# Chunked attention and two MoE layers: C loaded as half the bytes, in two transfers per unit into four tiles cleared once

## Chip, cores and metric

One core of one Trainium2 chip. The metric is the device time of one execution in microseconds (us), the median of several runs. The engines are TensorE (PE), VectorE (DVE), ScalarE (ACT), GpSimd (POOL) and SyncE (SP), which here only issues transfers.

## What is computed

Three layers in a row. The first is a chunked linear attention over x (4 batches, 8 heads, 768 steps, head size 32), with decays a and the projections B and C (16 numbers per step and head):

```python
for c in range(nc):
    cum = np.cumsum(la, axis=-1)
    L = np.exp(cum[:, :, :, None] - cum[:, :, None, :]) * causal
    CB = np.einsum('bhin,bhjn->bhij', Cc, Bc)
    y_intra = np.einsum('bhij,bhjd->bhid', CB * L, xc)
    y_inter = np.einsum('bhin,bhnd->bhid', Cc, state) * decay_to_i[:, :, :, None]
    y[:, :, sl] = y_intra + y_inter
    state = decay_full[:, :, None, None] * state + np.sum(Bx, axis=2)
```

The second is a gated MLP on the 3072 tokens (256 to 1536 and back, silu), the third routes each token to one of 8 experts (256 to 1024 and back, relu) by a gate with a bias per modality. C enters the first layer alone, in CB and in y_inter.

## The kernel before

The attention runs in 24 units (NU) of 128 steps of one batch with all 8 heads. A block is four units, 512 tokens; there are six, and the MLP of a block follows its four units. The order of all instructions is written out by hand: `first_block` (L807) has the setup, the loads of the first four units and the first two blocks, `block` (L950) the others, where the pieces of the next units are set between the groups of MLP matmuls. Each engine runs its own part of this order, one instruction after the other.

`load(u)` (L160) issues on SP's queue, for one unit, first xbb (256 KB: x, B by step, B transposed) and then cbd (256 KB: C). Both have four buffers, so unit u+4 is loaded when the values of unit u are done. In the first block SP's order is: at (L174), load(0), load(1), the rest of at (L812), load(2), weights 0 of the MLP (L391, 768 KB each), load(3), weights 1, and then load(u + 4) after each unit; the constants c1 go out on ACT's queue meanwhile (L175).

C comes as a block diagonal matrix, made on the host: a partition is one (group of 4 heads, head in the group, n), its free index (half of the unit, 4 heads, 64 steps), and all but the partition's own head are zeros. 64 KB of the 256 KB are numbers of C. `scores_mm` (L281) multiplies it with B transposed at L297, 64 partitions by 256 columns, so that each head meets only itself; `values_mm` (L331) multiplies single heads' 64 columns of it with the state at L353. `scores_m` (L301) masks the scores, `weigh` (L273) makes xw = x times a decay on POOL or DVE, `emit_d` and `emit_u` (L249, L264) make the decays du and U for a block. On POOL the order in the start is weigh(1), emit_d(0), emit_d(1), weigh(2), weigh(3), weigh(4). `decode` (L396) turns the packed weights into numbers on ACT and DVE (ha at L403); on ACT ha of the first weights stands ahead of the states st of unit 1 (L326, L327), which PE reads at L353.

`setup_ones` (L213) writes r16 and r32, the operands that sum or spread over groups of heads; r16 goes into cum_ends (L238).

Of the kernel before, what the change touches and what calls it, by code (L numbers as in the profile page):

```python
# [9 lines left out]
F32 = mybir.dt.float32  # L10
# [10 lines left out]
NB, NH, S, D, N = 4, 8, 768, 32, 16  # L21
NC = S // 128
NU = NB * NC
# [16 lines left out]
C_P8 = C_MU + 8  # L40
# [13 lines left out]
def _consts():  # L54
    k = np.arange(128)[:, None]
    j = np.arange(128)[None, :]
    c = np.zeros((128, C_END), np.float32)

    same = k // 64 == j // 64
    m = np.zeros((128, 128), np.float32)  # L60
    m[same & (k % 64 < 32) & (k > j)] = 1.0
    m[same & (k % 64 >= 32) & (k <= j)] = -1.0
    c[:, C_S:C_S + 128] = m
    for q, (lo, hi) in enumerate(((32, 96), (96, 128), (0, 32))):
        c[lo:hi, C_S + 128 + q] = -1.0
    r = np.arange(128)
    c[:, C_ME] = (r // 32) % 2
    for q in range(8):
        c[:, C_MU + q] = 4 * (r // 64) + (r // 8) % 4 == q
    c[:, C_P8:C_P8 + 8] = (r % 8)[:, None] == np.arange(8)[None, :]  # L70
    c[:, C_MK:C_MK + 64] = j[:, :64] >= k % 64
    c[:, C_ID:C_ID + 128] = k == j
    c[:, C_TRI:C_TRI + 128] = k < j
    e = np.arange(E)
    c[:, C_IE:C_IE + 8] = 8 - e
    for g, (b0, n) in enumerate(GROUPS):
        c[:, C_EC + 8 * g:C_EC + 8 * g + 8] = E * b0 * BLK + e * (n * BLK)
    c[:, C_LE:C_LE + 64] = (e[None, :] <= e[:, None]).reshape(1, 64)
    c[:, C_TT:C_TT + 11] = np.arange(11)
    c[:, C_KK:C_KK + 4] = np.arange(4) * BLK  # L80
    c[:, C_IO:C_IO + 8] = e
    return c


def _layout(inp):
    o = {}
    at = inp["a"].reshape(NB * NH, NC, 128).reshape(NB, NH, NC, 128).transpose(3, 0, 2, 1)
    o["at"] = at.reshape(128, NBLK, 32)
    xk = inp["x"].reshape(NB, NH, NC, 128, D).transpose(3, 0, 2, 1, 4).reshape(128, NU, DM)
    bk = inp["B"].reshape(NB, NH, NC, 128, N).transpose(3, 0, 2, 1, 4).reshape(128, NU, 128)  # L90
    bt = inp["B"].reshape(NB, NH, NC, 128, N).transpose(1, 4, 0, 2, 3).reshape(128, NU, 128)
    o["xbb"] = np.concatenate([xk, bk, bt], axis=2)

    ct = inp["C"].reshape(NB, 2, 4, NC, 2, 64, N).transpose(1, 2, 6, 0, 3, 4, 5).reshape(2, 4, N, NU, 2, 64)
    cd = np.zeros((2, 4, N, NU, 2, 4, 64), np.float32)
    for h in range(4):
        cd[:, h, :, :, :, h] = ct[:, h]
    o["cbd"] = cd.reshape(128, NU, 512)
    o["cst"] = _consts()

    def bits(w):
        return np.ascontiguousarray(w).view(np.int64)

    wg = bits(inp["moe_w_gate"]).reshape(2, 128, NF, 128).transpose(2, 1, 0, 3)
    wv = bits(inp["moe_w_val"]).reshape(2, 128, NF, 128).transpose(2, 1, 0, 3)
    wo = bits(inp["moe_w_out"]).reshape(NF, 128, DM)
    o["mw"] = np.concatenate([wg.reshape(NF, 128, 256), wv.reshape(NF, 128, 256), wo], axis=2)
    o["mid"] = np.ascontiguousarray(inp["moe2_modality_id"]).reshape(NU, 128).T
    o["wl"] = inp["moe2_w_gate"].reshape(2, 128, E).transpose(1, 0, 2)
    o["mb"] = np.broadcast_to(inp["moe2_modality_bias"].reshape(1, 2, E), (128, 2, E))  # L110
    w1 = inp["moe2_w1"].reshape(E, 2, 128, F2).transpose(0, 2, 1, 3).reshape(E, 128, 2 * F2)
    w2 = inp["moe2_w2"].reshape(E, NF2, 128, DM).transpose(0, 2, 1, 3).reshape(E, 128, NF2 * DM)
    o["ew"] = np.concatenate([w1, w2], axis=2).reshape(E * 128, 4096)
    return {k: np.ascontiguousarray(v) for k, v in o.items()}
# [3 lines left out]
def kernel(  # L118
# [5 lines left out]
    nc = tc.nc  # L124
# [6 lines left out]
    ap_ = att_stack.enter_context(tc.tile_pool(name="ap", bufs=1, side="right"))  # L131

    def ps_a(shape, name):
        return ps.tile(shape, F32, tag="a", bufs=3, name=name)

    def ps_g(name, shape=(128, BLK)):
        return ps.tile(list(shape), F32, tag="g", bufs=3, name=name)
# [5 lines left out]
    c1 = ap_.tile([128, C1], F32, name="c1")  # L143
# [6 lines left out]
    r16 = ap_.tile([128, 128], F32R, name="r16")  # L150
    r32 = ap_.tile([128, 2, 128], F32R, name="r32")
    mk = c1[:, C_MK:C_MK + 64]
    raw = {}
    xt_t = {}
    y_t = {}
# [4 lines left out]
    def load(u):  # L160
        if u >= NU or u in raw:
            return
        r = {}
        xbb = ap_.tile([128, 512], F32, name="xbb", tag="xbb", bufs=4)
        nc.sync.dma_start(out=xbb, in_=I["xbb"][:, u])
        r["x"] = xbb[:, 0:DM].rearrange("k (h d) -> k h d", h=8)
        r["b"] = xbb[:, DM:DM + 128]
        r["bt"] = xbb[:, DM + 128:]
        r["c"] = ap_.tile([128, 2, 4, 64], F32, name="cbd", tag="cbd", bufs=4)
        nc.sync.dma_start(out=r["c"].rearrange("p r h i -> p (r h i)"), in_=I["cbd"][:, u])  # L170
        raw[u] = r

    def setup_loads():
        nc.sync.dma_start(out=at0[:, 0:2], in_=I["at"][:, 0:2])  # L174
        nc.scalar.dma_start(out=c1, in_=I["cst"][:, 0:C1])  # L175
        nc.scalar.preload_act_table_set("natural_log_exp_and_others")

    def setup_ln(b0, b1):
        a = at[:, b0:b1]
        nc.vector.tensor_scalar(out=a, in0=at0[:, b0:b1].unsqueeze(2).to_broadcast([128, b1 - b0, 2, 32]),  # L180
                                scalar1=1e-6, scalar2=1.0, op0=ALU.max, op1=ALU.min)
        nc.scalar.activation(out=a, in_=a, func=AF.Ln)
# [28 lines left out]
        nc.scalar.activation(out=t, in_=c1[:, C_ME:C_ME + 1], func=AF.Silu)  # L211

    def setup_ones():  # L213
        p8 = c1[:, C_P8:C_P8 + 8].unsqueeze(2)
        nc.vector.tensor_copy(out=r16.rearrange("p (h n) -> p h n", h=8), in_=p8.to_broadcast([128, 8, 16]))
        nc.vector.tensor_copy(out=r32.rearrange("p g (h i) -> p (g h) i", h=4), in_=p8.to_broadcast([128, 8, 32]))

    def cum_split(b0, n):
# [62 lines left out]
    def scores_mm(u):  # L281


        r = raw[u]
        r["pc"] = [ps_a([128, 512], "pc") for _ in range(2)]
        r["pS"] = [p[:, 256:320] for p in r["pc"]]
        for q in range(4):
            for i in range(2):
                if i == 0 or u % NC != NC - 1:
                    k = slice(64 * i, 64 * i + 64)  # L290
                    nc.tensor.matmul(out=r["pS"][i][32 * q:32 * q + 32], lhsT=r["b"][k, 32 * q:32 * q + 32],  # L291
                                     rhs=r["xw"][k, 2 * q:2 * q + 2], start=True, stop=True,
                                     tile_position=(64 * i, 32 * q))
        for q in range(4):
            for g in range(2):
                k = slice(64 * g, 64 * g + 64)
                nc.tensor.matmul(out=r["pc"][g][32 * q:32 * q + 32, 0:256], lhsT=r["bt"][k, 32 * q:32 * q + 32],  # L297
                                 rhs=r["c"][k, q // 2].rearrange("p h i -> p (h i)"), start=True, stop=True,
                                 tile_position=(64 * g, 32 * q))

    def scores_m(u):  # L301
# [29 lines left out]
    def values_mm(u):  # L331

        r = raw[u]
        st = s_t.pop(u)
        py = r["py"] = [ps_a([128, 192], "py"), ps_g("py", (128, 192))]
        for g in range(2):
            for q in range(4):
                for i in range(2):  # L340
                    k = slice(64 * i, 64 * i + 64)

                    nc.tensor.matmul(out=py[i][32 * q:32 * q + 32, 128 * g:128 * g + 64], lhsT=r["xw"][k, 4 * g + q],  # L343
                                     rhs=r["m"][k, g, q], start=g == 0, stop=True, tile_position=(64 * i, 32 * q),
                                     skip_group_check=True)
        for half in range(2):
            if half == 0 and u % NC == 0:
                continue
            for q in range(4):
                for g in range(2):  # L350
                    k = slice(64 * g, 64 * g + 64)
                    o = 64 * (half + g)
                    nc.tensor.matmul(out=py[g][32 * q:32 * q + 32, o:o + 64],  # L353
                                     lhsT=st[k, half, 32 * (q % 2):32 * (q % 2) + 32], rhs=r["c"][k, half, q],
                                     start=False, stop=True, tile_position=(64 * g, 32 * q), skip_group_check=True)

    def values_out(u):
# [743 lines left out]
    with tc.For_i(bounds[0], bounds[1], 1) as t:  # L1101
        r = Routed(2, t, hl_t[0], None)
# [34 lines left out]
```

## Time and profile before

| what | value |
|---|---|
| median of 3 runs | 530.3 us (530.1 to 530.32) |
| the profiled execution's own time | 530.17 us |
| its span in the profile | 528.4 us |
| PE matmul busy | 505.0 us, 96% of the span |
| DVE, ACT, POOL busy | 289.1, 219.5, 105.8 us |
| transfers | 45.55 MB, 86 GB/s over the span |
| xbb and cbd | 24 transfers each, 256 KB |

The profile is of one execution. Times in it are us from the start of the span, where not marked ns. A line L297 is line 297 of the kernel. A busy PE is not PE at its peak: matmuls overlap, and their ends are modelled. Who released a wait is inferred from semaphore events. "issue" is time in which an engine waited for nothing that the profile shows. SPq is SP's queue, PEld PE's weight loads, PEldq its queue.

### The profile page before, as it was taken

How to read it: one execution, taken by the hardware profiler on the slowest of the kernel's cores; microseconds unless marked ns; L12 is line 12 of the kernel's file. 1: busy time of each engine (PE TensorE's matmuls, PEld its weight loads, DVE VectorE, ACT ScalarE, POOL GpSimd, SP SyncE). 2: the span in 40 equal slices, each digit the busy share in tenths (PEclk: the TensorE clock that was granted, in tenths of full speed). 3: DMA queues.
4: the chain of work that ended last, by engine and by line, in shares of the span. 5: the costliest groups of instructions: out<-in, count | busy, mean ns of one | idle time of the engine just before them, and what ended most of it. 6: DMA issues, size and time to landing. Idle time of an engine off the chain costs nothing.

```text
span 528.4 us, 11243 instructions
## 1 busy us (share of the span) xinstructions
PE 505.0 (96%) x4580; PEld 416.7 (79%) x4580; DVE 289.1 (55%) x631; ACT 219.5 (42%) x403; POOL 105.8 (20%) x127
## 2 busy tenths in 40 slices
PE   6889999999999999999999999999999999999990
PEld 3677787778788778888788778888899989999880
DVE  4998786944554544445444554455466564646320
ACT  4785575434333334233333332434454353534220
POOL 3200000220220130005000224211055426240220
PEclk9999999999999999999999999999999999999995
DMA  8954422011230312012100104234188544521100
GB/s 299 338 183 137 155 80 82 25 49 41 82 32 30 103 15 66 3 47 74 21 2 2 43 1 158 84 121 41 41 105 176 162 130 137 153 104 42 40 22 22
DMA packets 20694, 45.55 MB, mean 86 GB/s; under 512 B 4768, under 2 KB 8352, under 8 KB 20640
## 3 DMA queue, kind: packets, MB, share of 16 engines
q1 hardware_dynamic: 17424, 38.29, 26.2%
q0 software_dynamic: 3072, 6.41, 4.1%
q8 instruction: 37, 0.61, 0.6%
q14 instruction: 17, 0.14, 0.1%
q10 hardware_dynamic: 144, 0.11, 0.1%
HBM read 38.30 MB, written 6.50 MB: 85 GB/s over the span
## 4 chain that ended last, share of the span: by engine, by line
PE 76%; issue 11%; DVE 4%; POOL 3%; ACT 2%; DMA 1%; SPq 0%; POOLq 0%; DVEq 0%; ACTq 0%
PE py L469 19%; PE pg L441 18%; PE pv L441 18%; PE ph L758 7%; PE po L779 6%; PE pt L553 2%; POOL out L793 2%; PE pc L297 2%; PE py L353 1%; PE py L343 1%; PE pc L291 1%; DMA xbb<-in_xbb 1%; PE pu L270 1%; DVE wv L412 1%; PE px L747 1%
## 5 line engine op out<-in xcount | busy, mean ns | idle before, releaser
L441 PE MATMUL pg<-xt,wh 128*128 128x512 f32 x288 | 93.2, 404 | 0.3 <-ACT xt L374 0.2
L441 PE MATMUL pv<-xt,wh 128*128 128x512 f32 x288 | 90.4, 395 | 0.0
L449 DVE TENSOR_TENSOR h<-h,pv 128x512 f32<-128x512 f32 x72 | 49.4, 686 | 66.7 <-PE pv L441 55.6
L456 DVE TENSOR_TENSOR hl<-h,hh 128x512 fp32r<-128x512 f32 x72 | 50.2, 697 | 61.7 <-ACT hh L455 61.5
L758 PE MATMUL ph<-xt,hl 128*128 128x512 f32 x288 | 72.7, 394 | 0.0
L779 PE MATMUL po<-hl,hh 128*128 128x256 f32 x384 | 70.1, 283 | 0.0
L441 PEld LDWEIGHTS pv<-xt,wh 128*128 128x128 f32 x288 | 54.2, 188 | 12.8
L779 PEld LDWEIGHTS po<-hl,hh 128*128 128x128 f32 x384 | 60.3, 188 | 2.1
L455 ACT CAST hh<-h 128x512 fp32r<-128x512 f32 x72 | 44.6, 620 | 40.4 <-DVE h L449 40.4
L441 PEld LDWEIGHTS pg<-xt,wh 128*128 128x128 f32 x288 | 52.1, 188 | 11.6 <-ACT xt L374 0.6
L448 ACT ACTIVATE h<-pg 128x512 f32<-128x512 f32 x72 | 42.7, 593 | 41.7 <-PE pg L441 41.7
L614 POOL DMA_INDIRECT slots<-ids,si x24 | 26.0, 1081 | 168.4 <-DVE si L606 163.6
L758 PEld LDWEIGHTS ph<-xt,hl 128*128 128x128 f32 x288 | 51.7, 188 | 9.2
L469 PE MATMUL py<-hh,wh 128*128 128x512 f32 x144 | 58.7, 407 | 0.0
L441 PE MATMUL pg<-xt,wl 128*128 128x512 f32 x144 | 57.0, 396 | 0.3 <-DVE wl L421 0.3
L469 PE MATMUL py<-hl,wh 128*128 128x512 f32 x144 | 56.9, 395 | 0.0
L469 PE MATMUL py<-hh,wl 128*128 128x512 f32 x144 | 56.8, 394 | 0.0
L441 PE MATMUL pv<-xt,wl 128*128 128x512 f32 x144 | 56.8, 394 | 0.0
L779 PE MATMUL po<-hl,hl 128*128 128x256 f32 x192 | 53.9, 281 | 0.2 <-DVE hl L767 0.2
L767 DVE SCALAR_TENSOR_TENSOR hl<-ph,hh 128x512 fp32r<-128x512 f32 x48 | 33.0, 688 | 31.8 <-ACT hh L766 30.8
L766 ACT ACTIVATE hh<-ph 128x512 fp32r<-128x512 f32 x48 | 28.8, 600 | 41.4 <-PE ph L758 24.3
L779 PEld LDWEIGHTS po<-hl,hl 128*128 128x128 f32 x192 | 36.1, 188 | 0.4 <-DVE hl L767 0.4
(140 smaller groups left out, 669.6 us busy)
## 6 DMA issues: line engine op xcount, KB each, us to landing
eraw<-in_ew SPq DMA_DIRECT2D x24, 512.0 KB
wraw<-in_mw SPq DMA_DIRECT2D x12, 768.0 KB
xbb<-in_xbb SPq DMA_DIRECT2D x24, 256.0 KB
cbd<-in_cbd SPq DMA_DIRECT2D x24, 256.0 KB
yd<-yr SPq DMA_DIRECT2D x6, 528.0 KB
slots<-ids,si POOLq DMA_INDIRECT x24
xg<-yd,idx POOLq DMA_INDIRECT x24
out<-ob,idx POOLq DMA_INDIRECT x24
```

Source lines behind the costliest of these rows:

```text
L297: nc.tensor.matmul(out=r["pc"][g][32 * q:32 * q + 32, 0:256], lhsT=r["bt"][k, 32 * q:32 * q + 32], rhs=r["c"][k, q // 2].rearrange("p h i ...
L441: nc.tensor.matmul(out=t, lhsT=w[:, f, o:o + 128], rhs=xt[:, xp, k, cs], start=n == 0, stop=n == 5)
L448: nc.scalar.activation(out=h, in_=p[0], func=AF.Silu)
L449: nc.vector.tensor_tensor(out=h, in0=h, in1=p[1], op=ALU.mult)
L455: nc.scalar.copy(out=hh, in_=h)
L456: e.tensor_tensor(out=hl, in0=h, in1=hh.bitcast(F32), op=ALU.subtract)
L469: nc.tensor.matmul(out=yb[b][d][:, c:c + m], lhsT=w[:, f, o:o + 128], rhs=h, start=first and n == 0, stop=last and n == 2, skip_group_chec ...
L614: i = nc.gpsimd.indirect_dma_start(out=slots[0:E * upto], out_offset=bass.IndirectOffsetOnAxis(ap=si[:, s:s + 1], axis=0), in_=ids[g][:, o ...
L758: nc.tensor.matmul(out=p, lhsT=self.hl[:, w, o:o + 128], rhs=self.xt[:, xp, k], start=n == 0, stop=n == 5)
L766: nc.scalar.activation(out=hh, in_=p, func=AF.Relu)
L767: nc.vector.scalar_tensor_tensor(out=hl, in0=p, scalar=0.0, in1=hh.bitcast(F32), op0=ALU.max, op1=ALU.subtract)
L779: nc.tensor.matmul(out=self.po[s // 2][:, s % 2], lhsT=h[:, q], rhs=self.hl[:, w, o:o + DM], start=f == 0 and n == 0 and s % 2 == 0, stop= ...
```

## The change

On the host the heads are ordered anew. A partition is now (group of 4 heads, pair p, n, t), where t says whether the head is odd, and its 256 numbers are (p, half of the unit, 64 steps) with zeros only where p is not the partition's own pair: 128 KB per unit, half of them zeros. On the chip the tile still has 512 numbers per partition, [4, 2, 64], of which a partition with t = 0 uses the first 256 and one with t = 1 the last 256; the others are zero. So there are four tiles made once, cleared by a memset each on POOL in `setup_loads`, and `load` fills them by two transfers of 64 rows of 1 KB: one into every other partition's first half, one into the others' second half. The matmuls read their columns with a step (scores: four runs of 64) or at another place (values); B, r16 and the index into the masked scores follow the new order of heads. The host's layout of B and C in `_layout` is left out here.

```diff
+    cbd = [ap_.tile([128, 4, 2, 64], F32, name=f"cbd{i}") for i in range(4)]
...
-        r["c"] = ap_.tile([128, 2, 4, 64], F32, name="cbd", tag="cbd", bufs=4)
-        nc.sync.dma_start(out=r["c"].rearrange("p r h i -> p (r h i)"), in_=I["cbd"][:, u])
+        r["c"] = cbd[u % 4]
+        for t in range(2):
+            nc.sync.dma_start(out=r["c"].rearrange("(r t) a c i -> t r (a c i)", t=2)[t, :, 256 * t:256 * t + 256],
+                        in_=I["ct"][:, u].rearrange("(r t) j -> t r j", t=2)[t])
...
         nc.scalar.preload_act_table_set("natural_log_exp_and_others")
+        for t in cbd:
+            nc.gpsimd.memset(t, 0.0)
...
+        p8 = c1[:, C_P8:C_P8 + 8].rearrange("p (q t) -> p q t", q=4).unsqueeze(2)
+        nc.vector.tensor_copy(out=r16.rearrange("p (q n t) -> p q n t", q=4, t=2), in_=p8.to_broadcast([128, 4, 16, 2]))
         p8 = c1[:, C_P8:C_P8 + 8].unsqueeze(2)
-        nc.vector.tensor_copy(out=r16.rearrange("p (h n) -> p h n", h=8), in_=p8.to_broadcast([128, 8, 16]))
...
-                                 rhs=r["c"][k, q // 2].rearrange("p h i -> p (h i)"), start=True, stop=True,
+                                 rhs=r["c"][k, :, q // 2], start=True, stop=True,
...
-                                     rhs=r["m"][k, g, q], start=g == 0, stop=True, tile_position=(64 * i, 32 * q),
+                                     rhs=r["m"][k, g, 2 * (q % 2) + q // 2], start=g == 0, stop=True, tile_position=(64 * i, 32 * q),
...
-                                     lhsT=st[k, half, 32 * (q % 2):32 * (q % 2) + 32], rhs=r["c"][k, half, q],
+                                     lhsT=st[k, half, 32 * (q % 2):32 * (q % 2) + 32], rhs=r["c"][k, 2 * (q % 2) + q // 2, half],
```

## Rows read from the trace of the kernel before

**Rows 1.** The page: busy tenths of PE in 40 equal slices of the span.

```profile
PE   6889999999999999999999999999999999999990
```

**Rows 2.** Stretches: us, busy us of each engine (instructions), PEclk, DMA share, GB/s.

```profile
2.00:26.00 24.00, 18.80 (x435) 12.49 (x436) 17.07 (x55) 14.01 (x32) 7.02 (x8) 1.00 0.97 342
...
53.00:520.00 467.00, 460.79 (x3706) 384.58 (x3705) 247.51 (x527) 185.98 (x341) 98.57 (x115) 1.00 0.27 70
```

**Rows 3.** The chain that ended last, 0 to 18 us: start us, us, what.

```profile
2.10 4.36 DMA xbb<-in_xbb
...
8.27 1.22 PE pu L270 x2
...
15.05 0.85 issue
...
16.66 0.39 ACT er L195
```

**Rows 4.** Waits: us in total, times, longest us; 0 to 60 us, then SP's queue.

```profile
POOL xw L278 <- DMA xbb<-in_xbb: 10.9, 3, 6.2
...
SPq L391 <- DMA xbb<-in_xbb: 0.3, 1, 0.3
```

**Rows 5.** Timeline: start us, us, engine, line, what xcount [idle before <-releaser].

```profile
2.79 0.23 DVE L180 TENSOR_SCALAR at<-at 128x128 f32<-128x128 f32 x1 [2.79 <-DMA at<-in_at]
...
6.61 0.61 POOL L278 TENSOR_TENSOR xw<-xbb,W 128x256 f32<-128x256 f32 x1 [6.17 <-DMA xbb<-in_xbb]
...
11.24 0.92 ACT L403 ACTIVATE ha<-wraw 128x768 f32<-128x768 f32 x1 [0.75 <-DMA wraw<-in_mw]
...
12.01 0.62 POOL L278 TENSOR_TENSOR xw<-xbb,W 128x256 f32<-128x256 f32 x1 [2.09 <-DMA xbb<-in_xbb]
...
12.06 0.33 ACT L326 ACTIVATE st<-se,eb 128x64 f32<-128x64 f32 x1
...
14.07 0.35 PE L353 MATMUL py<-cbd,st 64*32 64x64 f32 x3
```

**Rows 6.** Stretches of the start, columns as in rows 2.

```profile
4.00:6.00 2.00, 1.77 (x35) 0.80 (x34) 1.39 (x6) 0.50 (x2) 0.00 (x0) 1.00 0.96 264
11.00:12.00 1.00, 1.00 (x33) 0.75 (x19) 0.96 (x4) 0.76 (x1) 0.00 (x0) 1.00 1.05 426
13.00:14.00 1.00, 1.00 (x47) 0.59 (x32) 0.53 (x1) 1.00 (x3) 0.00 (x0) 1.00 1.02 385
```

**Rows 7.** Timeline of SP's queue: start us, us, what it issued.

```profile
0.72 0.39 SPq L174 DMA_DIRECT2D at<-in_at  x1
...
1.64 0.42 SPq L170 DMA_DIRECT2D cbd<-in_cbd  x1
2.10 0.46 SPq L165 DMA_DIRECT2D xbb<-in_xbb  x1
...
4.51 0.43 SPq L391 DMA_DIRECT2D wraw<-in_mw  x1
...
6.48 0.33 SPq L391 DMA_DIRECT2D wraw<-in_mw  x1
```

**Rows 8.** POOL's memsets among the groups by line: busy us, mean ns.

```profile
L1001 POOL MEMSET xg<- 128x1056 f32 x2 | 1.9, 978 | 8.8 <-PE pg L441 8.8
...
L501 POOL MEMSET tmp<- 128x128 int32 x1 | 0.2, 208 | 74.7 <-DVE wv L412 74.7
```

**Rows 9.** Lines L204, L441, then L291, L297 from 53 us: ns min/median/max.

```profile
L204 PE MATMUL pi<-r x14: 387/396/504, 16.4 to 23.8; 128*128 128x512 f32 x14
...
L441 PE MATMUL pg<-xt,wh x288: 390/393/503, 24.4 to 367.0; 128*128 128x512 f32 x144
...
L291 PEldq EVENT_SEMAPHORE  x16: 51/51/51, 84.4 to 291.8; - x16
...
  issue: 5.5, 15
...
L297 PE MATMUL pc<-cbd,xbb x240: 376/376/400, 88.8 to 296.5; 64*32 64x256 f32 x120
```

More of the change, by code (lines that the diff above doesn't have):

```diff
@@ L89, in _layout @@
     xk = inp["x"].reshape(NB, NH, NC, 128, D).transpose(3, 0, 2, 1, 4).reshape(128, NU, DM)
-    bk = inp["B"].reshape(NB, NH, NC, 128, N).transpose(3, 0, 2, 1, 4).reshape(128, NU, 128)
-    bt = inp["B"].reshape(NB, NH, NC, 128, N).transpose(1, 4, 0, 2, 3).reshape(128, NU, 128)
+    bq = inp["B"].reshape(NB, 4, 2, NC, 128, N)
+    bk = bq.transpose(4, 0, 3, 1, 5, 2).reshape(128, NU, 128)
+    bt = bq.transpose(1, 5, 2, 0, 3, 4).reshape(128, NU, 128)
     o["xbb"] = np.concatenate([xk, bk, bt], axis=2)
[L94 to L98, printed above, removed]
+    ct = inp["C"].reshape(NB, 2, 2, 2, NC, 128, N).transpose(1, 2, 6, 3, 0, 4, 5).reshape(2, 2, N, 2, NU, 128)
+    cd = np.zeros((2, 2, N, 2, NU, 2, 128), np.float32)
+    for p in range(2):
+        cd[:, p, :, :, :, p] = ct[:, p]
+    o["ct"] = cd.reshape(128, NU, 256)
     o["cst"] = _consts()
```

## The prediction

> **What bounds the kernel now.** I began with the 40 slices of the page [rows 1]: TensorE (PE) stands at 9, that is 90% or more, from the fourth slice to the last but one. The stretches say the same in us [rows 2]: from 53 to 520 us PE works 460.8 of 467 us with the DMA engines at a share of 0.27. A lighter load of C is worth nothing there; only an instruction that PE itself runs longer or waits longer for would be felt. So the gain has to come before 53 us. The DMA side is full from 2 to 26 us: share 0.97, 342 GB/s, with PE at work 18.8 of 24 us.
>
> In that first part I read the chain of waits [rows 3]. One transfer is on it: xbb of unit 1, issued at 2.10 us, landed 4.36 us later. GpSimd (POOL) then weighs x and makes du, PE starts at 8.27 us with pu and goes from block to block until ScalarE (ACT) takes over at 16.66 us. From there to the solid stretch the chain is work of ACT and VectorE (DVE) in their own order, with no transfer in it, so a shift of that landing is a shift of the end, as far as nothing else takes its place. The waits [rows 4] agree: POOL stood still three times for an xbb, 10.9 us in all, 6.2 the longest. The next one ends at 12.01 us, for unit 3 [rows 5], and is not on the chain.
>
> **Part 1: fewer bytes.** A unit's C falls from 256 KB to 128 KB in as many rows, 128, of 1 KB instead of 2 KB. What a 1 KB row costs no row shows, so I bound it. Where nearly all rows are of 2 KB (13 to 14 us) the engines move 385 GB/s at a full share, where they are of 6 KB mostly (11 to 12 us) 426 at a share of 1.05, so some 405 [rows 6]. Sixteen engines then take 85 ns for 2 KB and 243 ns for 6 KB, 0.0386 ns a byte and 6 ns a row: about 46 ns for 1 KB. The saving per unit is 128 x 39 ns / 16 = 0.31 us at that pace. From 4 to 6 us, when the transfers in question run, the pace was 264 GB/s [rows 6]; 128 KB less at that pace are 0.50 us. Only one C transfer (unit 0's) stands ahead of xbb of unit 1. I take 0.4 us: the landing moves from 6.46 to about 6.05 us. Ends: 0 (the landing is set by something else) and 1.2 (below).
>
> The same saving for units 1 and 2 brings the weights of the MLP, 384 KB less ahead of them, up to 1.1 us forward at 342 GB/s; ACT waited 0.75 us for them before ha at 11.24 us [rows 5]. That is worth nothing by itself: behind ha on ACT stands st at 12.06 us, which PE reads at 14.07 us, so there is 1.4 us of slack.
>
> **Part 2: one more issue per unit.** SP issues a transfer every 0.47 us or so in the start (at 1.64 and 2.10 us, to take two [rows 7]). With two for C, xbb of unit 1 is issued at 2.57 us. Does it then come too late for its place in the queue? The shortest way from issue to use in the trace is the first transfer, `at`: issued at 0.72 us, used by DVE at 2.79 us [rows 7, 5], 2.07 us for 32 KB. Add 224 KB more at 264 to 385 GB/s (0.6 to 0.85 us) and xbb of unit 1 could land at 5.25 to 5.5 us; the queue lets it land at 6.05. So the later issue is covered by the queue, with 0.5 us to spare; without that cover it costs 0.47 us. The same 5.25 us is the furthest end of part 1 (6.46 - 5.25 = 1.2).
>
> The weights, three issues later, go out at 5.9 instead of 4.51 us and xbb of unit 3 behind them at about 6.4; before, POOL had that one at 12.01 us, long after it was issued, so it too stood in the queue. One more row matters here: the second weight transfer went at 6.48 us, after a wait of 0.3 us that ended when xbb of unit 1 landed [rows 4, 7]. It is the eighth issue after that one and shares no tile with it: an issue waits for the one eight before it. With three issues a unit, eight reach back 2.7 units instead of four. Followed through, the weights would wait for the second half of C of unit 0 (about 4.7 us, before 5.9), xbb of unit 3 for xbb of unit 1 (6.05, before 6.4), later ones likewise. The first transfer of weights, 768 KB, keeps the engines busy meanwhile. Cost 0. Later a unit's loads are issued four units before their use, in a stretch that PE fills: 0.33 us more on SP cost 0.
>
> A page of the Trainium skill speaks against this part. The row shows 4.36 us from the issue of xbb to its landing, far more than its 256 KB need at 342 GB/s (0.77 us), so it mostly stood in the queue. DMA: Bandwidth & Descriptors, "Anatomy of one DMA — SWDGE (gpsimd) path", gives a transfer a fixed part of some 2.0 us, setup and confirmation, to which bytes add little; the 2.07 us of `at` agree. By it alone, halving a transfer saves hardly anything and the later issue is paid in full: +0.47 instead of -0.4 us.
>
> **Part 3: the four clears on POOL.** Each is 512 floats per partition. The two memsets of the trace are 1056 elements in 978 ns and 128 in 208 ns [rows 8]; in between, 527 ns each, 2.1 us for four, and by the ends 0.8 and 3.9 us. POOL has nothing until 6.61 us [rows 5], so they are done by about 2.8 (at worst 4.6) us if they begin with the first issue, at 0.72. SP's first C transfer waits for the first clear, due at about 1.25 us, before its issue at 1.64; at 978 ns each the clears still end at about 1.7, 2.7 and 3.7 us, against issues at 1.64, 3.04 and 4.9 us. Cost 0 (at most 0.1).
>
> **Part 4: PE.** The C operand of the score matmuls becomes four runs of 64 columns instead of one of 256. The stepped operand of the trace, twice 256 columns at L204, takes 396 ns (median) where the plain 512 of L441 take 393 [rows 9]: 0. A unit's scores now depend on two transfers, so PE's queue may get one more semaphore instruction per unit: 51 ns each [rows 9]. Of the 24 units fifteen have their scores after 53 us (240 matmuls at L297, 16 a unit [rows 9]): between 0 and 0.8 us. There are already 16 such instructions at L291 for these fifteen units, and PE stood 5.5 us "issue" in 15 times before these groups, 0.37 us each, in which a queue that runs ahead can do it. I take 0 and keep 0.8 for the range. The stepped copy in setup_ones has as many elements as before, beside DVE work that is not on the chain: 0.
>
> **Sum.** 530.17 us of the profiled execution - 0.4 = 529.8 us. That execution lies 0.13 us under the median of 530.3, so the sum is not against an odd one. A difference under 0.2%, 1.06 us, can't be told from none here, so I call this the same.
>
> **Rivals.**
> *Hidden or issue-bound.* The landing of xbb is set by its own issue, or by one late engine, and the clear, the second issue and PE's extra wait show: 530.2 to 530.6, with the wait on PE up to 531.4. For it: 4.36 us is long for 256 KB. Against: share 0.96 from 4 to 6 us. Chance 0.19.
> *A larger gain.* xbb lands as early as it can (-1.2), and the 0.85 us in which PE stood "issue" at 15.05 us in the middle of the chain [rows 3] shrinks since less is queued: down to -2.05, 528.1. Against: nothing ties that gap to data transfers. Chance 0.16, of which nearly all passes -1.06.
> *Slower: the halves in series.* The second half of a C tile is issued only when the first has landed, since both write one tile. It decides as soon as SP waits at the second half of unit 0. The first half can't land before about 4.0 us (1.64 + 2.07 + some queue), so xbb of unit 1 goes at 4.6 and lands at about 7.4 (+0.9), and the weights, with two more such waits ahead, go at about 11.5 and land past 14, against 11.24. ACT stands at ha for 3 us and holds st, PE and all that follows: about +3, 533.2. Against: the halves touch different columns and different partitions. Chance 0.08.
> *Slower by PE.* The extra semaphore costs PE about 0.1 us a unit because what it loads behind it starts late: 24 x 0.1 - 0.4 = +2.0, 532.2. It decides above 0.06 us a unit. Chance 0.05.
> The forecast keeps 0.52. Faster 0.16, same 0.71 (forecast and the first rival), slower 0.13. The range, 528.9 to 531.4, takes in -1.25 and the wait on PE with an issue-bound landing.
>
> **What would show it.** Right: POOL's xw of unit 1 starts at about 6.2 instead of 6.61 us and pu at about 7.9 instead of 8.27; the chain reaches the solid stretch 0.4 us earlier; SP shows three issues a unit 0.47 us apart, PE about 0.37 us before each score group, as now. Wrong: a long SP wait between the two halves; score groups longer after 53 us; POOL's xw at 6.6 or later; PE's gap at 15 us gone.

## The result, and the profile after

The changed kernel takes **534.79 us** (median of 4 runs, 532.15 to 535.21) where the kernel before takes 530.31: ratio **1.0077 [1.0048, 1.0105]**. Forecast were 529.8 us and "the same"; it is slower, above the range.

| | before | after |
|---|---|---|
| median, us | 530.31 | 534.79 |
| the profiled execution's own time, its span | 530.17, 528.4 | 532.15, 530.0 |
| PE matmul busy, us | 505.0 | 505.4 |
| MB moved | 45.55 | 42.41 |
| first matmul of the MLP (pg, L441; after: L448) | 24.40 us | 24.93 us |
| last matmul of PE | 513.99 us | 515.34 us |

The trace after is that of the fastest of these runs, so it accounts for only 1.6 us of the 4.5: 0.5 us of span lost by 25 us, of which 0.2 come back by 248 us, 1.0 lost at 252.8 us, and 0.3 behind the last matmul. What the other runs lose beyond that stands at the end of the part on the prediction. I begin with the start, in the order of [rows 2 to 8]. The stretches (columns as in [rows 2]):

```profile
2.00:26.00 24.00, 18.53 (x433) 12.29 (x434) 17.68 (x53) 13.92 (x30) 7.80 (x10) 1.00 0.86 289
...
4.00:6.00 2.00, 1.77 (x36) 1.12 (x36) 1.05 (x4) 0.51 (x2) 0.00 (x0) 1.00 0.70 201
6.00:8.00 2.00, 1.11 (x18) 0.46 (x3) 1.93 (x8) 0.00 (x0) 2.00 (x3) 1.00 0.73 218
8.00:10.00 2.00, 2.00 (x34) 0.98 (x42) 1.01 (x3) 1.34 (x3) 1.48 (x2) 1.00 0.81 258
```

The DMA engines were full in the start, share 0.97 [rows 2, 6]; now they stand at 0.70 to 0.81 from 4 to 10 us. The bytes saved have become idle time of the engines. SP's queue tells why (start us, us, what it issued):

```profile
0.73 0.40 SPq L178 DMA_DIRECT2D at<-in_at  x1
1.19 0.43 SPq L167 DMA_DIRECT2D xbb<-in_xbb  x1
1.68 1.19 SPq L173 DMA_DIRECT2D cbd<-in_ct  x2
2.91 0.59 SPq L167 DMA_DIRECT2D xbb<-in_xbb  x1
3.54 1.11 SPq L173 DMA_DIRECT2D cbd<-in_ct  x2
...
7.03 0.58 SPq L398 DMA_DIRECT2D wraw<-in_mw  x1
...
9.35 0.58 SPq L398 DMA_DIRECT2D wraw<-in_mw  x1
```

The two halves of C hold SP for 1.1 to 1.2 us together, where the one transfer held it for 0.43 [rows 7], and the transfer right behind them holds it for 0.59 instead of 0.46. The weights go out at 7.03 us instead of 4.51. POOL's waits (us in total, times, longest), the timeline, and the chain that ended last:

```profile
POOL xw L285 <- DMA xbb<-in_xbb: 9.9, 3, 3.6
```

```profile
0.73 1.91 POOL L182 MEMSET cbd<- 128x512 f32 x4 [0.29 <-POOLq L1134]
6.00 0.77 POOL L285 TENSOR_TENSOR xw<-xbb,W 128x256 f32<-128x256 f32 x1 [3.37 <-DMA xbb<-in_xbb]
11.52 0.92 ACT L410 ACTIVATE ha<-wraw 128x768 f32<-128x768 f32 x1 [1.48 <-DMA wraw<-in_mw]
13.75 0.96 DVE L419 SCALAR_TENSOR_TENSOR wv<-ha,wv 128x768 int32<-128x768 int32 x1 [1.37 <-ACT wv L413]
16.59 0.62 POOL L285 TENSOR_TENSOR xw<-xbb,W 128x256 f32<-128x256 f32 x1 [3.57 <-DMA xbb<-in_xbb]
16.72 0.63 DVE L379 TENSOR_TENSOR y<-y,z 128x128 f32<-128x128 f32 x1
24.93 0.96 PE L448 MATMUL pg<-xt,wh 128*128 128x512 f32 x2 [1.83 <-ACT xt L381]
```

```profile
7.03 4.47 DMA wraw<-in_mw
...
11.52 0.92 ACT ha L410
...
12.91 0.81 ACT wv L413
...
17.35 0.88 DVE wv L423
...
18.25 0.83 ACT wh L426
...
24.51 0.38 ACT xt L381
```

xbb of unit 1 did come earlier: POOL takes it at 6.00 us instead of 6.61 [rows 5], its longest wait for an xbb is 3.6 us instead of 6.2 [rows 4], and PE runs 0.45 us ahead of the kernel before up to 14 us and about 1 us ahead at 22 us. But the chain now begins with the weights. ha starts 0.28 us later than before [rows 5], DVE waits 1.37 us for ACT's wv, and PE, ahead of its time, waits 1.83 us for xt: it has gained a microsecond and waits it off, and the solid stretch begins 0.5 us late.

ha gives only 0.28 us of that. The rest comes in at DVE's y of L379 (L372 before), which takes 0.63 us here and took 0.28 before:

```profile
16.45 0.28 DVE L372 TENSOR_TENSOR y<-y,z 128x128 f32<-128x128 f32 x1
16.65 0.95 DVE L416 SCALAR_TENSOR_TENSOR wv<-wraw,wv 128x768 int32<-128x768 int32 x1
17.72 0.83 ACT L419 CAST wh<-wv 128x768 fp32r<-128x768 f32 x1
```

It runs beside POOL's xw of unit 4, whose xbb was issued at 10.04 instead of 7.25 us and landed later: that xw starts at 16.59 instead of 15.26 us. In all 16 traces a y of this line that begins in the first 22 us while POOL is at work ends only after POOL's instruction has ended. So DVE's wv, 0.28 us late until then, is 0.62 us late behind it (17.27 against 16.65 us).

The second loss stands in the middle of that stretch, where nothing was expected (PE's timeline; the gap is on the chain as well):

```profile
252.63 0.36 PE L360 MATMUL py<-cbd,st 64*32 64x64 f32 x15
253.70 0.43 PE L360 MATMUL py<-cbd,st 64*32 64x64 f32 x13 [0.70 <-issue]
```

PE stands still between two of 28 like matmuls, for 0.92 us from one start to the next, with no semaphore in between. From the last long matmul ahead of this group (scores of unit 20, values of unit 19) to the first behind it, the kernel before takes 1.7 us, this one 2.7. Two rows of the page and two of the groups of L304 go with it:

```profile
PE 505.4 (95%) x4580; PEld 417.6 (79%) x4580; DVE 290.9 (55%) x631; ACT 219.6 (41%) x403; POOL 108.0 (20%) x131
...
q8 instruction: 37, 0.61, 0.5%
```

```profile
L304 PE MATMUL pc<-cbd,xbb x384: 372/376/631, 5.4 to 297.8; 64*32 64x256 f32 x192
L304 PEldq EVENT_SEMAPHORE  x24: 51/51/51, 5.3 to 295.1; - x24
```

The second pair answers to [rows 9]: the stepped operand takes 376 ns as before, and PE has one semaphore instruction more per unit. The first pair: 37 loads of 16 KB on the instruction queue for some 9,200 instructions of PE are one for every 250, so I take them for PE loading its program as it goes. One such load begins at 253.1 us, in the middle of the standstill.

### The profile page after: what moved, and what is told of

Its sections match the earlier page's. It is cut to its first block, busy times and chain, and to the rows that moved or that the text cites. A ratio compares the mean times of both kernels' runs of the same rounds, so it can differ in the third digit from the quotient of the medians.

```text
span 530.0 us, 11314 instructions
## 1 busy us (share of the span) xinstructions
PE 505.4 (95%) x4580; PEld 417.6 (79%) x4580; DVE 290.9 (55%) x631; ACT 219.6 (41%) x403; POOL 108.0 (20%) x131
## 2 busy tenths in 40 slices
DMA packets 21078, 42.41 MB, mean 80 GB/s; under 512 B 5152, under 2 KB 11808, under 8 KB 21024
## 4 chain that ended last, share of the span: by engine, by line
PE 77%; issue 9%; DVE 5%; ACT 2%; POOL 2%; DMA 1%; SPq 1%; POOLq 0%; DVEq 0%
PE py L476 18%; PE pg L448 18%; PE pv L448 18%; PE ph L765 8%; PE po L786 8%; PE pt L560 2%; POOL out L800 1%; PE pc L304 1%; PE py L360 1%; PE py L350 1%; DVE wv L419 1%; DMA wraw<-in_mw 1%; PE px L754 1%; PE pc L298 1%; DVE wv L423 1%
## 5 line engine op out<-in xcount | busy, mean ns | idle before, releaser
L448 PE MATMUL pg<-xt,wh 128*128 128x512 f32 x288 | 93.1, 404 | 1.9 <-ACT xt L381 1.8
L448 PE MATMUL pv<-xt,wh 128*128 128x512 f32 x288 | 90.4, 395 | 0.0
L448 PEld LDWEIGHTS pv<-xt,wh 128*128 128x128 f32 x288 | 54.2, 188 | 12.7
L448 PEld LDWEIGHTS pg<-xt,wh 128*128 128x128 f32 x288 | 52.2, 189 | 13.1 <-ACT xt L381 2.3
L448 PE MATMUL pg<-xt,wl 128*128 128x512 f32 x144 | 57.0, 396 | 0.3 <-DVE wl L428 0.3
L448 PE MATMUL pv<-xt,wl 128*128 128x512 f32 x144 | 56.8, 394 | 0.0
```

The costliest lines, as they stand in the source:

```text
L448: nc.tensor.matmul(out=t, lhsT=w[:, f, o:o + 128], rhs=xt[:, xp, k, cs], start=n == 0, stop=n == 5)
```

## The experiments

Three theories at first. **I**: SP's issues, and with them the weights' landing, come too late; the loss is before 30 us. **P**: PE is held up after 53 us. **L**: the clears and the new layout cost. A shift of the solid stretch is read at the first MLP matmul (24.40 us before), a standstill as the time between two starts inside a unit's small matmuls.

**again**: the changed kernel, unchanged.

> The changed kernel once more, for a second trace and more times. Its first trace lost only 1.6 us of span on the kernel before, while the median of its runs lost 4.5 us. Theory I (issues): the loss arises before 30 us, because SP hands out the transfers of 64 rows more slowly (0.59 us each) and the first weights land later; then a slower run should show the weights landing later still and ACT's ha past 11.5 us, and the solid stretch beginning 2 us or more late. Theory P (PE): the loss arises after 53 us, in stops of PE like the one of 0.9 us at 252.7 us; then a slower run should show several of them and no later begin of the solid stretch. Expected 532 to 535.5 us.

Measured: 533.05 us (532.5 to 533.74), ratio 1.0055 [1.0041, 1.0069]. The trace repeats both losses: first MLP matmul 24.98 us, PE stands still 1.34 us at 252.85 us. Neither is an accident of one execution.

**two_full**: the kernel before, with its 256 KB of C split by rows only; no clear, no new layout, no byte saved.

```diff
-        nc.sync.dma_start(out=r["c"].rearrange("p r h i -> p (r h i)"), in_=I["cbd"][:, u])
+        for t in range(2):
+            nc.sync.dma_start(out=r["c"].rearrange("(r t) a h i -> t r (a h i)", t=2)[t],
+                              in_=I["cbd"][:, u].rearrange("(r t) j -> t r j", t=2)[t])
```

> The kernel before, with the C transfer split alone: two transfers of 64 alternate rows of 2 KB, all 256 KB, no clear, no new layout. Theory I: as slow as the changed kernel or slower, 533 to 537 us, with the first weights issued near 7 us instead of 4.51. Theory P (one more semaphore on PE's queue per unit): also slower, 531 to 535, but with the solid stretch beginning within 1 us of before. A theory L, that the clear or the stepped operand costs: 530.3, as before.

Measured: 536.07 us, ratio 1.0115 [1.01, 1.0131]. From its timeline:

```profile
6.95 0.58 SPq L393 DMA_DIRECT2D wraw<-in_mw  x1
...
14.15 0.89 ACT L405 ACTIVATE ha<-wraw 128x768 f32<-128x768 f32 x1 [3.52 <-DMA wraw<-in_mw]
27.34 0.96 PE L443 MATMUL pg<-xt,wh 128*128 128x512 f32 x2 [1.04 <-ACT xt L376]
256.17 0.59 PE L355 MATMUL py<-cbd,st 64*32 64x64 f32 x9 [0.75 <-issue]
```

The split alone makes both losses, the first more than five times as large (+2.9 us). No byte was saved here, and still the DMA engines stand at shares of 0.76 to 0.88 from 4 to 14 us, as they would if SP hands out too little. (The granted clock is at its lower level, 0.5, from 17.6 us for 3.4 us, so a part of the 2.9 us may be the clock's.) L falls.

**one_half**: the changed kernel with one transfer of 128 rows of 1 KB per unit; C of the odd heads goes to the wrong columns.

```diff
-        for t in range(2):
-            nc.sync.dma_start(out=r["c"].rearrange("(r t) a c i -> t r (a c i)", t=2)[t, :, 256 * t:256 * t + 256],
-                        in_=I["ct"][:, u].rearrange("(r t) j -> t r j", t=2)[t])
+        nc.sync.dma_start(out=r["c"].rearrange("p a c i -> p (a c i)")[:, 0:256], in_=I["ct"][:, u])
```

> The changed kernel with one transfer of 128 rows of 1 KB into the first half of each tile (it leaves the odd heads' numbers of C in the wrong columns, so the attention's result is another): half the bytes, one issue. Theory I: the gain that was forecast, 529.3 to 530.2 us, the first weights issued near 4.6 us. Theory P: 530.0 to 530.4. Theory L: as slow as the changed kernel, 532 to 535.

Measured: 530.67 us, ratio 1.001 [1.0001, 1.0019]; no standstill after 53 us, and a time above what either theory had for it. In the start:

```profile
4.48 0.43 SPq L396 DMA_DIRECT2D wraw<-in_mw  x1
...
11.94 0.92 ACT L408 ACTIVATE ha<-wraw 128x768 f32<-128x768 f32 x1 [1.90 <-DMA wraw<-in_mw]
25.01 0.96 PE L446 MATMUL pg<-xt,wh 128*128 128x512 f32 x2 [1.51 <-ACT xt L379]
```

Half the bytes, as many issues as before, and still no gain: ha starts 0.7 us later [rows 5] although the weights are issued as before, and the solid stretch waits for them (1.51 us for xt). The second weights go out at 6.02 instead of 6.48 us and so share the engines longer with the first; that this is the reason is argued, not shown.

**whole_first4**: the changed kernel, but units 0 to 3 get C whole in one 256 KB transfer from a host copy of the full tile; no clear.

> The changed kernel, but units 0 to 3 are loaded whole, zeros included, in one transfer of 256 KB as before (so no clear); two transfers of 64 rows from unit 4 on. Theory I: the start is as before, 530.0 to 531.2 us. Theory P: 532 to 535, since the units after 53 us are as in the changed kernel.

Measured: 534.12 us, ratio 1.0074 [1.006, 1.0088]. For the start theory I had a beginning as before, and that is a miss:

```profile
4.51 0.43 SPq L402 DMA_DIRECT2D wraw<-in_mw  x1
...
11.82 0.91 ACT L414 ACTIVATE ha<-wraw 128x768 f32<-128x768 f32 x1 [0.76 <-DMA wraw<-in_mw]
...
25.05 0.95 PE L452 MATMUL pg<-xt,wh 128*128 128x512 f32 x2 [0.34 <-ACT xt L385]
```

Up to 12 us SP issues one transfer for C, at 128 rows, and the first weights leave at 4.51 us as before. Still ha starts 0.58 us late and the solid stretch 0.65 us late, as late as in the changed kernel. So the late issues can't be all of the loss in the start; why these weights land later isn't known.

Its standstill is of another kind, and it shows what comes after (timeline, then stretches):

```profile
153.16 1.66 SPq L179 DMA_DIRECT2D cbd<-in_ct  x2
153.21 0.36 DVE L380 TENSOR_TENSOR y<-py,U 128x192 f32<-128x192 f32 x1 [3.89 <-PE pg L452]
...
156.30 0.79 PE L480 MATMUL py<-hh,wh 128*128 128x512 f32 x1 [2.17 <-DVE yT L552]
```

```profile
153.70:156.30 2.60, 0.43 (x2) 0.00 (x0) 1.61 (x6) 1.17 (x3) 0.00 (x0) 1.00 0.56 43
156.30:159.70 3.40, 3.40 (x10) 2.82 (x11) 2.69 (x7) 0.83 (x2) 0.00 (x0) 0.51 0.31 83
```

The last small matmul of that group (values of unit 12, scores of unit 13) starts at 149.5 us. Both who wait for its end, DVE's y and SP's next load of C, go on only at 153.2, 3.7 us later; in the kernel before both do so 0.24 to 0.36 us after the last start, in all groups after 53 us:

```profile
149.26 0.36 DVE L369 TENSOR_TENSOR y<-py,U 128x192 f32<-128x192 f32 x1 [0.47 <-PE py L353]
```

PE's signal came late, and PE then waited for DVE. I call such a late signal, or a standstill without a semaphore, a hold-up. The semaphore that counts PE's finished matmuls shows the same: no step between 149.64 and 153.15 us, in which the trace has long matmuls start on PE, and then five within 0.2 us. After the standstill the granted clock is 0.51, the lower level, for 3.4 us: at half speed they cost 1.7 us more. PE is 4.5 us behind, 0.6 of it from the start.

**shift20**: a new theory for the second loss, the *place*: the extra semaphore instructions push PE's program so that a load of it falls into a run of small matmuls. Test: the kernel before, ten of the 14 warm-up matmuls (L204) split in two.

```diff
-        for _ in range(n):
+        for _ in range(n - m):
...
+        for i in range(2 * m):
+            nc.tensor.matmul(out=idle_t[0][:, i % 2], lhsT=r32[:, 0], rhs=r32.rearrange("p g j -> p (g j)"),
+                             start=True, stop=True)
...
-            keep_busy((0, 4, 4, 6)[u])
+            keep_busy((0, 4, 4, 6)[u], (0, 2, 4, 4)[u])
```

> The kernel before, in which ten of the fourteen warm-up matmuls of PE between 17 and 24 us (512 columns each) are split into two of 256 columns: the same columns and products, 20 more PE instructions, nothing else; no transfer differs. That is the number of instructions by which PE's program is longer in the changed kernel when it comes to its standstill at 252.8 us. Theory of the place (the changed kernel's PE stops at 252.8 us because the added instructions put the loading of the next piece of PE's program into a run of small matmuls): PE stands still 0.9 to 2.6 us, 'issue', near 252 us, and the time is 531.0 to 533, ratio 1.0015 to 1.005. Theory of the transfers (the stop comes of the added transfers, which disturb the loading of the program): no standstill, 530.1 to 530.6, ratio within 0.0006 of 1.

Measured: 530.26 us, ratio 0.9996 [0.9987, 1.0005], no standstill, all 11 runs within 529.93 to 530.59. The place alone does not do it.

**after_shift28**: the changed kernel with the same edit for all 14.

> The changed kernel with all fourteen warm-up matmuls split in two: 28 more PE instructions from 24 us on, nothing else. Theory of the place: the standstill at 252.8 us (L360 of the changed kernel) is gone or stands at another time; if no other run of small matmuls is hit, the loss after 53 us is 0 and the time about 531.1 (the start's +0.6 stays), ratio 1.001 to 1.002; if another is hit, as much as the changed kernel or more, with the standstill elsewhere. Theory of the transfers: standstill at 252 to 254 us as in the changed kernel, 532.5 to 535.

Measured: 531.85 us, ratio 1.0027 [1.0017, 1.0037]; no standstill, first MLP matmul at 25.35 us. That would fit the place; but the signal of that same group is late here too: DVE takes y at 255.2 us, 1.8 us after the last small matmul. The hold-up is there, but PE runs over it with long matmuls. In the start ha comes at 12.30 us, 0.8 later than in the changed kernel, though up to there the two issue the same transfers at the same times: the landing of the weights differs by that much between executions, so 0.28 us in one trace say little by themselves. Over all, the four traces with this start have ha at 11.50 to 12.30 us, the three with the old one at 11.24 to 11.37.

**weights_first** and **before_weights_first**: the first weights issued ahead of unit 2's loads, in the changed kernel and, as a control, in the kernel before.

```diff
-        load(2)
         load_w(0)
+        load(2)
```

> The changed kernel with the first weights of the MLP issued ahead of unit 2's loads (at about 5.3 instead of 7.03 us). Theory of the issues (in the changed kernel SP issues too slowly, the DMA engines run partly dry from 4 to 10 us, and the weights' landing at 11.5 us starts the chain that sets the end of the start): weights land by 10.5 us, ACT's ha starts 0.7 us or more earlier than 11.52, and the solid stretch of PE begins 0.4 to 1.2 us earlier than in the changed kernel, at or ahead of the kernel before; the standstill at 252.8 us stays, so the time is 0.4 to 1.2 us under the changed kernel's of this chip. Rival (something else holds the chain from 17 us on, or unit 2's loads, now later, do): the solid stretch begins where it does in the changed kernel or later, and the time is equal or higher.

> The control: the kernel before with the first weights issued ahead of unit 2's loads (3.6 instead of 4.51 us). There the DMA engines are full from 2 to 14 us, so the weights can gain what stood ahead of them, 512 KB at 342 to 400 GB/s, about 1.3 us, and unit 2's loads lose 2 us. Theory of the issues: ha 1 us earlier than 11.24; if the weights' landing is what sets the chain already in the kernel before, the solid stretch begins up to 0.5 us earlier and the time is 529.8 to 530.2; if the chain stands on xbb and DVE's own work as the prediction had it, no gain, 530.2 to 530.6, or a loss where unit 2's xbb (POOL took it at 12.01 us, the chain does not) comes late.

Measured: 535.91 us (533.07 to 539.12), ratio 1.0115 [1.0082, 1.0147]; control 530.79, ratio 1.0003 [0.9994, 1.0012]. From the first one's timeline, and its chain:

```profile
5.33 0.43 SPq L398 DMA_DIRECT2D wraw<-in_mw  x1
...
10.25 0.91 ACT L410 ACTIVATE ha<-wraw 128x768 f32<-128x768 f32 x1 [0.20 <-DMA wraw<-in_mw]
24.50 0.95 PE L448 MATMUL pg<-xt,wh 128*128 128x512 f32 x2
```

```profile
19.19 2.42 issue
```

The start behaves as theory I has it: ha 1.27 us earlier, the solid stretch 0.43 us earlier. The control gains nothing (ha at 10.33 us, first MLP matmul at 24.65): before the change the weights were not what held it. PE stood still 2.64 us at 18.98 us, on the chain, so no more was gained. The time is higher for another reason: at 252.5 us PE stands still twice, 1.27 and 0.62 us, and the clock is at its lower level from 255.5 to 258.9 us (granted 0.50). The expectation of a lower time was a miss.

**weights_shift28**, and once more as **both_again**: both edits in the changed kernel.

> The changed kernel with both edits at once: the first weights issued ahead of unit 2's loads, and all fourteen warm-up matmuls split in two (28 more PE instructions, so that the standstill at 252.8 us should be gone). If the loss of the changed kernel is the sum of two independent parts (weights landing late, PE's standstill in unit 20's small matmuls), both are taken out: solid stretch within 0.3 us of the kernel before, no standstill of over 0.3 us after 53 us, 530.2 to 530.9, ratio 0.9995 to 1.001. Rival (a third cost in the changed kernel, such as the stepped operand or the semaphores themselves): 531.3 or more with neither of the two in the trace.

> The changed kernel with first weights ahead of unit 2's loads and all warm-up matmuls split, a second time. The first time its runs lay in two groups, 529.9 to 530.1 and 531.0 to 532.3. If the groups belong to the kernel, they come again (medians 529.9 to 531.5); the theory of the two costs says that the lower group is the kernel without a standstill (about 0.5 us under the kernel before) and that an execution of the upper group shows a standstill of PE or a stretch at half clock.

Measured: 531.03 us, ratio 1.0008 [0.9996, 1.002], and 530.59, ratio 1.0006 [0.9994, 1.0018]. The first profile has no standstill, the first MLP matmul at 23.85 us and a span of 527.8 us, 0.6 under the kernel before: with both losses out, this one execution has the half microsecond that was forecast. The medians don't. The second stands still 1.15 us at 252.4 us, begins at 24.43, and has a span of 529.5. So this kernel's runs spread (529.7 to 533.7), and the shift doesn't rule the standstill out. The place theory falls with it.

**two_block_place**: the kernel before, C in two blocks of 64 neighbouring rows, which different matmuls read, so that PE gets no extra semaphore instruction in the group; nine warm-up matmuls split, to have the group at 252 us where it is in the changed kernel's program.

> The kernel before with C's 256 KB loaded in two transfers of 64 neighbouring rows (the two groups of heads) instead of one of 128; nine warm-up matmuls split in two, so that unit 20's small matmuls lie at the same place of PE's program as in the changed kernel. Each half is read by matmuls of its own, so PE gets no extra semaphore instruction in the group. Two questions. Issue: if SP's 0.59 us per issue comes of every other row, these issues take 0.43 to 0.48 us, the weights go out at about 5.9 us and the solid stretch starts 0 to 1.2 us later than before; if it comes of 64 rows, they take 0.55 to 0.6 us, the weights go at about 6.9 us, and it starts 2 to 3 us later, as in the kernel with whole rows split in two. Standstill: theory of the transfers, PE stands still at 252 to 256 us in unit 20 (0.8 to 2 us); theory that the extra semaphore instruction is needed for it, no standstill after 53 us. Times: 530.3 to 531.5 with cheap issues and no standstill, 533 to 536 with dear issues and a standstill, the mixed cases between.

Measured: 536.05 us, ratio 1.0102 [1.0086, 1.0118].

```profile
1.67 1.20 SPq L171 DMA_DIRECT2D cbd<-in_cbd  x2
2.91 0.59 SPq L165 DMA_DIRECT2D xbb<-in_xbb  x1
...
257.73 0.64 PE L358 MATMUL py<-cbd,st 64*32 64x64 f32 x16 [1.38 <-issue]
```

Both questions are answered: neighbouring rows cost SP the same 1.2 us for two, so it is the 64 rows and not their spacing; and PE stands still (1.6 us) without the extra semaphore.

**spare_transfer**: shift20, and from unit 4 on 64 rows of C more into a tile that nothing reads.

> The kernel before with ten warm-up matmuls split (unit 20's small matmuls at the same place of PE's program as in the changed kernel; that alone showed no standstill) and, from unit 4 on, one transfer more per unit: 64 rows of 1 KB of C into a tile that nothing reads. C itself still comes in one transfer, so the start, PE's waits and PE's program are those of that kernel. Theory that place and number of transfers together make the standstill, whatever PE waits for: PE stands still 0.8 to 2 us at 252 to 254 us, 531.2 to 533.5, ratio 1.0015 to 1.006. Theory that it takes a transfer for which PE itself waits (C in halves): no standstill after 53 us, 530.1 to 530.8.

Measured: 533.0 us, ratio 1.0058 [1.0043, 1.0073]. Not at 252 us, but as in whole_first4: y comes 3.24 us after the last small matmul of the group at 149 us, and PE stands still 2.13 us at 153.77.

```profile
152.81 0.36 DVE L376 TENSOR_TENSOR y<-py,U 128x192 f32<-128x192 f32 x1 [3.45 <-PE pg L448]
...
155.90 0.50 PE L476 MATMUL py<-hh,wh 128*128 128x512 f32 x1 [1.73 <-DVE yT L548]
```

One useless transfer per unit costs 2.7 us, with C, layout and PE's program as they were. In the trace 2.0 us of it are this hold-up and 0.7 the start (first MLP matmul at 25.16 against 24.46 in shift20), where PE stands still 2.13 us at 20.2 us (1.31 in shift20).

**act_half**, **act_half_weights**: the second half of C issued by ScalarE from unit 8 on, without and with the weights first.

```diff
-            nc.sync.dma_start(out=r["c"].rearrange("(r t) a c i -> t r (a c i)", t=2)[t, :, 256 * t:256 * t + 256],
+            e = nc.scalar if t and u > 7 else nc.sync
+            e.dma_start(out=r["c"].rearrange("(r t) a c i -> t r (a c i)", t=2)[t, :, 256 * t:256 * t + 256],
                         in_=I["ct"][:, u].rearrange("(r t) j -> t r j", t=2)[t])
```

> The changed kernel in which, from unit 8 on, the second half of C is issued on ScalarE's queue instead of SP's. As many transfers, bytes, waits of PE and PE instructions within one; SP issues one transfer less per unit, as in the kernel before. Theory of the queue (the standstills of PE at 153 or 252 us come of what stands on SP's queue, more issues or later ones): no standstill of over 0.3 us after 53 us, about 530.8 to 531.3, the start's +0.5 alone. Theory of the transfers (it is their number, wherever they are issued): a standstill at 153 or 252 us as in the changed kernel, 532 to 535. If ScalarE's issues cost it, groups of MLP would wait for ACT: PE's waits for ACT rise after 53 us.

> The same with the first weights issued ahead of unit 2's loads as well. If both theories hold (start: weights; later: SP's queue), neither loss is left: 529.7 to 530.4, at or under the kernel before. Theory of the transfers: 532 to 536, with the standstill.

Measured: 536.51 us, ratio 1.0114 [1.0099, 1.0128], standing still 1.51 and 0.92 us at 253.5 us, granted clock 0.50 behind it; and 534.99 us, ratio 1.0075 [1.0062, 1.0088], 1.26 and 1.98 us at 252.6 us. It isn't the additional issue on SP's queue.

**All profiles together.** Twelve kernels or repetitions have two transfers of C per unit (or the spare one). In each, the group at 149 or the one at 252 us shows a standstill of PE of 0.9 us or more, or DVE's y over 1.6 us after the last small matmul. In the four with one transfer (before, one_half, shift20, before_weights_first) y comes 0.24 to 0.29 us after it in both groups and PE runs through. In two of them, one_half and before_weights_first, y is 1.5 and 1.9 us late in the group at 194 us, where it costs nothing: hold-ups exist without a second transfer too. What is shown: a second transfer per unit, whoever issues it, whatever its layout, and whether PE waits for it or not, brings one at one of two places of the long stretch where it can cost time. What stays open is why: the loads of PE's program begin at these times (153 and 253 us) in the kernels without a hold-up too, and I have no run that holds these loads and the transfers apart.

## Why the prediction was wrong

**Part 1, xbb: right.** POOL's xw forecast at about 6.2 us, came at 6.00; pu at about 7.9, came at 7.83 us. The gain of 0.4 us existed, and more.

Two steps failed: the slack of the weights in part 1, with the issues of part 2 behind it (0.5 us), and the cover of the later loads in part 2 (the larger part).

**Part 1, the weights: the step that failed first.** "That is worth nothing by itself: behind ha on ACT stands st at 12.06 us, which PE reads at 14.07 us, so there is 1.4 us of slack." I followed ha to the next thing that PE reads and stopped. Behind st on ACT stands wv, DVE's wv needs it, wh needs that, and the MLP begins with wh and xt. In the kernel before, DVE's wv of L416 ends at 17.60 us and wh begins at 17.72: the slack on this way was 0.1 us, not 1.4. Once PE's own work came earlier, this was the chain; half a microsecond of gain beside it could not reach the end.

**Part 2, the issues: mis-sized.** 0.47 us per issue was the pitch of 128 rows; two transfers of 64 rows take 1.19 or 1.11 us. The weights were due at 5.9 and went at 7.03 us. "The first transfer of weights ... keeps the engines busy meanwhile" assumed a queue that is never empty; it ran dry, at shares of 0.70 to 0.81. So the weights landed at 11.50, 0.3 us later than before, where 384 KB less ahead of them should have brought them forward. Term forecast: 0; measured in the start: +0.5 us net, after 0.45 us gained. How much of that is the issues' is open: two_full and two_block_place, with the same issues, lose 2.9 and 3.7 us there, and weights_first gets 0.43 us back; but whole_first4 loses 0.65 us without them.

The section of the Trainium skill weighed there (DMA: Bandwidth & Descriptors, "Anatomy of one DMA — SWDGE (gpsimd) path") has a fixed part of about 2.0 us for a transfer that GpSimd issues; here SP issues, and the 2.07 us of `at` agree with it all the same. "Saves hardly anything" was more than it says: by its rate for the bytes, 128 KB less are 0.3 us (an estimate from its figure). That the later issue is paid in full did not hold for xbb: issued 0.81 us later, it was used 0.61 earlier. For the weights the issue was paid in part: 2.5 us later out, 0.3 later in.

**Part 3: right.** Four clears took 1.91 us, 524 ns each by their group's mean, against 527 forecast, beside other work; two_full, without a clear, issues the weights no earlier (6.95 against 7.03 us).

**Part 4, PE: the terms right, the bound wrong.** The stepped operand and the semaphores cost nothing: 376 ns and 51 ns, with groups as long as before. But I bounded PE's loss after 53 us by 0.8 us, from the semaphores, and sought no other. The standstill (0.9 to 2.6 us at a time, with the lower clock behind it up to 1.7 more) comes of the transfers in a stretch where they seemed covered. Part 2 put them at nothing with the words "in a stretch that PE fills: 0.33 us more on SP cost 0". This is the other step that failed, and the dearer one: spare_transfer shows 2.0 us of it in its trace. The sentence names the cover, and the cover did not hold, since PE itself was hit.

**The rivals.** "Slower by PE" named the right engine and half the loss (532.2 us; that the profiled run took 532.15 is chance), with the wrong mechanism, a price per unit instead of one standstill. "The halves in series" did not come about: the second half is issued right behind the first. In "a larger gain" I wrote that nothing ties PE's gap at 15.05 us [rows 3] to data transfers. Counting PE's instructions in the traces up to such gaps puts them within one or two of the 449th in 12 and of the 705th in 8 of the 16 traces (before: 1.12 us at 14.78, 1.13 us at 20.12), at times that differ by 2 us and more; 256 apart, about one 16 KB load. (In six of the 12 at the 449th the profile puts the wait down to ACT's U; at the 705th it names no semaphore.) So I read these gaps as PE waiting for its program while the DMA engines are full, which is argued, not shown. In the changed kernel's trace the first is down to 0.51 us and the second gone, and that is how PE came to be a whole microsecond ahead: the rival's gain was there, and it too was waited off at wh and xt. The Trainium skill (Runtime: NRT & Kernel Launch, "Instruction fetch mechanics") has the program refilled in blocks of 16 KiB, 256 instructions, by a DMA queue of the engine's own, at a cost that is "mostly hidden". The 37 loads agree with the blocks; that the cost is hidden does not agree with gaps of over 1 us around the chain's "issue" [rows 3], if the loading is their cause, and by it alone there would be no standstill to look for.

The other runs of the changed kernel are 2.2 to 3.1 us above the profiled one, at a mean granted clock of 0.986 to 0.987 against 0.990. A longer standstill and a stretch at the lower clock behind it, as in whole_first4, weights_first and act_half, would explain it (3.4 us at half the clock lower the mean over 530 us by 0.003); there are no traces of these runs, so this is argued, not shown, and it is the larger part of the 4.5 us.

No version beats the kernel before beyond the measurement.

## What to carry to other kernels

Fewer bytes in more transfers were no saving here: price each new shape of transfer by itself, and look whether the DMA share stays as high afterwards. When a step of a chain comes earlier, follow every other input of the first busy stretch to its end, not to its next reader. And a transfer under a full PE need not be free: here it held up PE itself where small matmuls run.

## What was not expected of the hardware

- Two transfers of 64 rows (1 or 2 KB, neighbouring or every other) hold SP 1.1 to 1.2 us and the issue right behind them 0.59, of 128 rows 0.42 to 0.46 each in the same stretch.
- PE can stand still with no semaphore to wait for, 0.9 to 2.0 us in a group of small matmuls and up to 2.6 us at the 705th instruction of the program; the signal of a finished matmul can reach DVE and SP up to 3.7 us after its start, where 0.24 to 0.36 us are usual.
- DVE's y of L379 takes 0.21 to 0.28 us by itself and 0.63 beside POOL's xw (after, 16.72 us).
- Behind standstills of over 1 us the granted clock was at its lower level, 0.5, for 3.4 us in six traces (two_full from 17.6, two_block_place 18.0, whole_first4 156.3, weights_first 255.5, act_half 256.6, act_half_weights 22.2 and 257.7 us); not behind all of them.
